# Converting the first weight's float64 words: two VectorE operations and a sign matmul in place of three VectorE operations

## The chip, the cores and the metric

The kernel runs on one core of a Trainium2 chip. The metric is device time in microseconds (us) of one execution. The profiler's span, from the first to the last instruction, is a little shorter than that time. Engines are named as in the profile: PE is TensorE, DVE VectorE, ACT ScalarE, POOL GpSimd and SP SyncE.

## The reference

Attention over B=4 batches, H=8 heads, S=768 positions and D=64, with a local window of 96 positions, 8 global keys and a linear distance bias, followed by a two-layer feed-forward net on the 3072 token rows:

```python
scores = scale * np.matmul(q, k.transpose(0, 1, 3, 2))
keep = is_global | is_local
dist = np.where(is_global & ~is_local, float(n_local), np.abs(rel))
scores = np.where(keep, scores - slopes * dist, -1e9)
a = softmax(scores); x = np.matmul(a, v)            # (3072, 512)
h = x @ w_in                                        # w_in: 512 x 2048
g = np.where(h >= 1, h, np.where(h <= -1, 0, (h + 1) ** 2 / 4))
out = g @ w_out                                     # w_out: 2048 x 512
```

The weights w_in and w_out arrive as float64, everything else as float32.

## The kernel before, in words

**Weights.** Each weight comes in 16 pieces of 512 KB, loaded as pairs of 32-bit words (`w_load`, three raw buffers). `w_bits` makes float32 words of them on VectorE in three operations on 128x512 tiles: line 430 takes the high word, masks it and shifts it left by three, into a PSUM tile; line 436 takes sign and top exponent bit from the high word and ors them in; line 439 shifts the low word right by 29 and ors it in, into the SBUF tile `w_f`. Then ScalarE writes a scaled float16 high half (`w_hi`, line 452), ScalarE scales `w_f` in place (`w_scale`, line 458), and GpSimd subtracts the half from it, which leaves the low half (`w_lo`, line 463). The halves are `wih`, `wil` (w_in) and `woh`, `wol` (w_out). The matmuls run on such pairs of halves.

**Attention.** A unit is 128 rows of one batch, a half unit four of its heads. The first row block of every batch (four units) is done in float32 by the `first_*` functions. The later ones use float16 pairs: `conv_hi`, `conv_lo` (lines 710 and 711 on GpSimd) split q, k and v; line 757 does the scores on TensorE; line 560 adds bias and takes the extreme on VectorE (`masked`, 128x256, or 128x128 in the first units); line 573 does the exponential on ScalarE; lines 774 and 776 split the result into `ph`; a transposing DMA brings `ph` to `pt`; line 801 multiplies with v; line 630 normalises into `xs`. Lines 740 and 742 copy the global keys and values.

**Feed-forward.** A chunk is 256 token rows (two units). `ffn1` (line 936) is the first product, three matmuls of 256 columns for each 128x128 weight block; `gelu` (lines 1011 to 1024) is the activation, split in halves; `ffn2` (line 1047) is the second product, three matmuls of 512 columns for each piece of w_out (a triple). Chunks 0 and 1 are made of the four first units, chunk 2 of the units 4 and 5. Later chunks use a seven-product scheme (line 973) with mixed weights (`tsum`, `tt`) and mixed inputs (`xa`).

**Fillers.** `filler` (line 400, tiles `spare_*`) multiplies zeros into a free PSUM tile. Its result is not used.

**What sets the order.** Each engine runs its instructions in the order in which the program issues them. Every piece of work is entered in a list by `at(t, ...)`, and the table `PLACE` gives the place of each entry in the final order, by hand. `after(...)` only asserts that what a piece of work needs has been issued ahead of it. Tiles come from pools: in PSUM `ps_s` has 2 buffers, `ps_av` 1, `ps_h` 3 and `ps_o` 2; the words of `w_bits`, the fillers and the outputs of the products share `ps_h` and `ps_o`. The sixteen pieces of w_in are converted ahead of those of w_out. ffn1 of chunk 0 starts when the first pieces of w_in are done.

Of the kernel before, what the change touches and what calls it, by code (L numbers as in the profile page):

```python
# [9 lines left out]
F16 = mybir.dt.float16  # L10
# [41 lines left out]
CPRE = 0  # L52
PRODUCTS = ("p1", "p5", "p2", "p6", "p3", "p7", "p4")
NFILL = 90
WS = "d"
# [218 lines left out]
def fast_path(ctx, tc, q, k, v, nraw, nval, w_in, w_out, out, half, nm, rr, sq, worst, badi):  # L274
# [109 lines left out]
    def slope(own, h):  # L384
# [6 lines left out]
        if h % 4 == 0:  # L391
            obias[h // 4] = ttp.tile([P, 4, P], F32, tag="t", name=f"obias{h // 4}")
# [49 lines left out]
    def signed(n):  # L442
        return WS[n % len(WS)] == "s"

# [21 lines left out]
    def put_weight(n, t, tl):  # L466
# [4 lines left out]
        if signed(n):  # L471
            at(t + 2.7, w_sign, n)
            t += 1.2
# [923 lines left out]
```

## Time and profile before

| what | value |
|---|---|
| time, median of 3 runs | 616.25 us (614.4 to 617.4) |
| time of the profiled execution | 616.34 us |
| span of the profiled execution | 614.1 us |
| TensorE busy | 593.3 us, 97% |
| VectorE busy | 479.7 us, 78% |
| ScalarE busy | 425.8 us, 69% |
| GpSimd busy | 362.0 us, 59% |
| mean granted clock of TensorE | 0.997 |

The busy shares are means over stages with different limits, so a stage is read from its own stretch of the trace. Matmuls overlap in a row: their pitch, from start to start, is shorter than their busy time. The page's chain of the work that ended last holds a single step here (ScalarE's last output copy), so the limits are read from the windows, the groups of lines and the timeline.

### The profile page before, as it was taken

Reading aid. Unit: us, or ns where it says so; the run is one execution under the profiler, and the core shown is the slowest. Engines: PE = TensorE matmul, PEld = TensorE weight load, DVE = VectorE, ACT = ScalarE, POOL = GpSimd, SP = SyncE. Lnnn points to the kernel's source line nnn. Section 1 sums busy time; section 2 is a strip of 40 time slices with the busy share of each in tenths; the row PEclk is TensorE's granted clock in tenths of the full one; section 3 lists DMA queues with packets and bytes.
Section 4 is the critical chain, followed back from the end, with each engine's and each line's share of the span. In section 5 each row is a group of like instructions: output and inputs, shape, how many; then the busy total and the mean of one; then the engine's idle time right before and its main releaser. Section 6 shows DMA issues by size and latency. Waiting matters only on the chain. (4 is left out here: it accounts for less than half of the span.)

```text
span 614.1 us, 17482 instructions
## 1 busy us (share of the span) xinstructions
PE 593.3 (97%) x6990; PEld 426.4 (69%) x6990; DVE 479.7 (78%) x1187; ACT 425.8 (69%) x865; POOL 362.0 (59%) x369
## 2 busy tenths in 40 slices
PE   5999899998999999999999999999999999999997
PEld 3677687444884777876766866776876877777865
DVE  6799999989885797797879778878788788752570
ACT  3688688688885877987568767768777766653431
POOL 0156869969999986486348447258458345324220
PEclk9999899999999999999999999999999999999999
DMA  9454256795575537788859677687698596162001
GB/s 306 137 174 157 74 192 158 232 256 105 139 153 127 127 88 124 177 159 202 185 140 225 196 175 180 164 185 171 191 187 191 139 191 126 41 88 44 19 19 36
DMA packets 158984, 91.74 MB, mean 149 GB/s; under 512 B 122932, under 2 KB 139572, under 8 KB 158900
## 3 DMA queue, kind: packets, MB, share of 16 engines
q1 hardware_dynamic: 158896, 90.60, 61.6%
q8 instruction: 55, 0.90, 0.6%
q14 instruction: 29, 0.24, 0.1%
q10 hardware_dynamic: 4, 0.00, 0.0%
HBM read 54.53 MB, written 6.29 MB: 99 GB/s over the span
## 5 line engine op out<-in xcount | busy, mean ns | idle before, releaser
L1024 POOL TENSOR_TENSOR gl<-u,gh 128x512 f16<-128x512 f32 x88 | 110.8, 1265 | 110.4 <-ACT gh L1022 108.4
L1047 PE MATMUL o<-woh,gh 128*128 128x512 f16 (+1 forms) x368 | 136.3, 370 | 0.0
L1047 PE MATMUL o<-woh,gl 128*128 128x512 f16 (+1 forms) x368 | 136.1, 370 | 0.0
L1047 PE MATMUL o<-wol,gh 128*128 128x512 f16 (+1 forms) x368 | 136.1, 370 | 0.0
L973 PEld LDWEIGHTS <-tt 128*128 128x128 f16 x1728 | 100.3, 98 | 10.0
L1047 PEld LDWEIGHTS <-gh 128*128 128x128 f16 x736 | 65.9, 98 | 58.0
L573 ACT ACTIVATE z<-z,nm 128x256 f32<-128x256 f32 (+1 forms) x192 | 85.3, 480 | 15.0 <-DVE nm L560 15.0
L560 DVE CUSTOM_DVE_ANT_0 z<-s,bias 128x256 f32<-128x256 f32 x160 | 64.8, 413 | 17.8 <-PE s L757 17.8
L1022 ACT ACTIVATE gh<-u 128x512 f16<-128x512 f32 x88 | 54.6, 625 | 25.2 <-DVE u L1015 24.7
L973 PEld LDWEIGHTS <-wih 128*128 128x128 f16 x864 | 66.9, 98 | 4.5 <-DVE u L1015 0.3
L936 PE MATMUL h<-xt,wih 128*128 128x256 f16 x384 | 65.5, 277 | 4.1 <-DVE w_f L439 3.4
L1047 PEld LDWEIGHTS <-gl 128*128 128x128 f16 x368 | 36.0, 98 | 40.0
L776 DVE SCALAR_TENSOR_TENSOR ph<-z,ph 128x1024 f16<-128x1024 f32 x40 | 54.3, 1356 | 7.4 <-DMA pt<-ph 3.6
L936 PE MATMUL h<-xt,wil 128*128 128x256 f16 x192 | 53.1, 276 | 0.0
L494 DVE TENSOR_REDUCE sq<-c_raw 128x1 f32<-128x256 f32 x128 | 48.0, 407 | 1.8 <-DMA c_raw<-in_moe_w_out_dram 1.3
L936 PEld LDWEIGHTS <-wih 128*128 128x128 f16 x384 | 37.8, 99 | 10.4 <-issue 4.0
L973 PEld LDWEIGHTS <-wil 128*128 128x128 f16 x432 | 42.3, 98 | 0.0
L774 ACT ACTIVATE ph<-z 128x1024 f16<-128x1024 f32 x40 | 41.9, 1048 | 0.3
L463 POOL TENSOR_TENSOR wil<-w_f,wih 128x512 f16<-128x512 f32 x16 | 18.7, 1171 | 38.8 <-ACT w_f L458 38.8
L801 PEld LDWEIGHTS <-pt 128*128 128x128 f16 x960 | 34.2, 97 | 9.4 <-DMA pt<-ph 2.9
L973 PE MATMUL h_0a<-xtb,tt 128*128 128x128 f16 x648 | 40.6, 219 | 0.0
L973 PE MATMUL h_1a<-xtb,tt 128*128 128x128 f16 x648 | 40.6, 219 | 0.0
(178 smaller groups left out, 1349.7 us busy)
## 6 DMA issues: line engine op xcount, KB each, us to landing
w_raw<-in_moe_w_in_dram SPq DMA_DIRECT2D x16, 512.0 KB, 4.0
w_raw<-in_moe_w_out_dram SPq DMA_DIRECT2D x16, 512.0 KB, 4.5
c_raw<-in_moe_w_in_dram SPq DMA_DIRECT2D x32, 256.0 KB, 4.0
c_raw<-in_moe_w_out_dram SPq DMA_DIRECT2D x32, 256.0 KB, 3.6
kr<-in_k_dram SPq DMA_DIRECT2D x28, 256.0 KB, 3.9
vr<-in_v_dram SPq DMA_DIRECT2D x28, 256.0 KB, 3.6
qr<-in_q_dram SPq DMA_DIRECT2D x24, 256.0 KB, 4.2
out_dram<-ob SPq DMA_DIRECT2D x23, 256.0 KB, 2.1
```

Of the source, the lines that this page charges most:

```text
L463: nc.gpsimd.tensor_sub(lo, wf[n], hi)
L494: nc.vector.tensor_reduce(sq[:, col : col + 1], r, axis=AX.X, op=op, apply_absolute_value=True)
L560: nc.vector.tensor_tensor_reduce(out=p32[u, hf][:, hh, :], in0=pts[u, hf][hh // 2][:, hh % 2, 0:n], in1=obias[hf][:, hh, :] if own else bi ...
L573: nc.scalar.activation(z, z, AF.Exp, bias=nm[:, c : c + 1], scale=-1.0, **acc)
L774: nc.scalar.activation(ph, zf, AF.Copy, scale=SP_)
L776: nc.vector.scalar_tensor_tensor(ph, zf, SP_, phs[u, hf, 0], op0=ALU.mult, op1=ALU.subtract)
L801: nc.tensor.matmul(av[:, hh, :], pt[:, a, hh, kt, :], vt[:, c, 4 * hf + hh, :], start=(n == 0), stop=(n == 5),)
L936: nc.tensor.matmul(hp[:, e, :], w[:, dc, f], xt[:, a, dc, :], start=(n == 0), stop=(n == 3 * NDC - 1))
L973: nc.tensor.matmul(hp[:, m, :], w, xf(b, dc), start=(fresh and m == n == 0), stop=(m == 3 and n == 5), skip_group_check=not fresh,)
L1022: nc.scalar.activation(gt[c, g][0], us[c, g], AF.Copy)
L1024: nc.gpsimd.tensor_sub(gt[c, g][1], us[c, g], gt[c, g][0])
L1047: nc.tensor.matmul(os_[c, t][x], a[:, cs], w[:, f, ms], start=(n == 0 and i == 0), stop=(n == NFC - 1 and i == 2))
```

## The change

For the 16 pieces of w_in:

- ScalarE takes the sign of the raw high word, read as float32, into a float16 tile (`w_sign`, line 430 of the changed kernel). TensorE multiplies it by a constant matrix `twos`, -2 on the diagonal (`w_twos`, line 434), so that the PSUM tile holds the word of -2.0 or +2.0. One VectorE operation shifts the high word left by three and xors the PSUM word in (line 442). The final operation is as before (line 452 there).
- The in-place scaling moves from ScalarE to GpSimd (line 466 there).

The pieces of w_out keep their three operations and ScalarE's scaling. The table PLACE is new throughout, with 27 filler entries in the program where 86 stood. The ones column of a value block may be written ahead of its halves (`v_block`), and the mixing of inputs asks for its low half only where it uses it.

```diff
-CPRE = 0
+TWOS = range(16)
+PSCALE = range(16)
-WS = "d"
...
+        nc.vector.tensor_scalar(twos, ident, -2.0, None, op0=ALU.mult)
...
+    def bits_tile(n):
+        num, src, hi, lo = piece(n)
+        p, tag = (ps_o, "o") if num < NFC and num % 2 >= BODD else (ps_h, "h")
+        wbits[n] = p.tile([P, *hi.shape[1:]], F32, tag=tag, name=f"w{num}_bits")
+        return wbits[n]
+
+    def w_sign(n):
+        num, src, hi, lo = piece(n)
+        wsgn[n] = ggp.tile([P, *hi.shape[1:]], F16, tag="g", name=f"w{num}_sign")
+        nc.scalar.activation(wsgn[n], wraw[n][:, :, :, 1].bitcast(F32), AF.Sign)
+
+    def w_twos(n):
+        after("positions")
+        nc.tensor.matmul(bits_tile(n), twos, wsgn[n], start=True, stop=True)
+
     def w_bits(n, s):
...
+        t = (bits_tile(n) if s == 0 and n not in TWOS else wbits[n]).bitcast(I32)
+        if s == 0 and n in TWOS:
+            nc.vector.scalar_tensor_tensor(t, rh, 3, t, op0=ALU.logical_shift_left, op1=ALU.bitwise_xor)
+            did.add(("bits", n, 1))
+        elif s == 0:
             nc.vector.tensor_scalar(t, rh, 0x07FFFFFF, 3, op0=ALU.bitwise_and, op1=ALU.logical_shift_left)
...
     def w_scale(n):
...
+        if n in PSCALE:
+            nc.gpsimd.tensor_scalar(wf[n], wf[n], SW, 1.0, op0=ALU.mult, op1=ALU.mult)
+        else:
+            nc.scalar.activation(wf[n], wf[n], AF.Copy, scale=SW)
...
     def put_weight(n, t, tl):
         at(tl, w_load, n)
+        if n in TWOS:
+            at(t - 0.6, w_sign, n)
+            at(t, w_twos, n)
+        at(t + 0.1, w_bits, n, 0)
+        if n not in TWOS:
+            at(t + 1.13, w_bits, n, 1)
         at(t + 2.63, w_bits, n, 2)
```

**VectorE at a piece of w_in, among the first units.** Before, the three operations of a piece stand apart, with other work between:

```order
L430 TENSOR_SCALAR w4_bits_463<-w4_raw_357 128x512
L630 TENSOR_TENSOR xs0_284<-av1_1_454,rr_68 128x256
L436 SCALAR_TENSOR_TENSOR w4_bits_463<-w4_raw_357,w4_bits_463 128x512
L430 TENSOR_SCALAR w6_bits_482<-w6_raw_416 128x512
L653 TENSOR_TENSOR xt0_310<-xtp1_1_478,xt0_310 128x2x128
L583 TENSOR_SCALAR rr_68<-sums_122 128x4
L439 SCALAR_TENSOR_TENSOR w4_f32_501<-w4_raw_357,w4_bits_463 128x512
```

Now (line 442 is the xor, line 452 the final operation):

```order
L641 TENSOR_TENSOR xs0_315<-av1_0_442,rr_68 128x256
L442 SCALAR_TENSOR_TENSOR w5_bits_459<-w5_raw_401,w5_bits_459 128x512
L452 SCALAR_TENSOR_TENSOR w5_f32_474<-w5_raw_401,w5_bits_459 128x512
L600 RECIPROCAL rr_68<-rr_68 128x4
L664 TENSOR_TENSOR xt0_326<-xtp1_0_480,xt0_326 128x2x128
L442 SCALAR_TENSOR_TENSOR w7_bits_492<-w7_raw_437,w7_bits_492 128x512
L452 SCALAR_TENSOR_TENSOR w7_f32_510<-w7_raw_437,w7_bits_492 128x512
```

(The names carry the piece, w4 for piece 4.) The and-shift and the and-or of a piece have become one operation, and the final operation, which needs its result, now stands directly behind it.

**TensorE ahead of the first matmul of ffn1.** Before (line 400 is a filler, line 598 a transpose, line 936 ffn1):

```order
L400 MATMUL spare_o10_490<-zeros_120 128x512
L400 LDWEIGHTS zeros_120
L400 MATMUL spare_h21_492<-zeros_120 128x512
L400 LDWEIGHTS zeros_120
L400 MATMUL spare_o11_494<-zeros_120 128x512
L598 MATMUL tp2_0_496<-ident_119,z2_0_406 128x128 x4
L936 LDWEIGHTS wih_114
L936 MATMUL h0_0_508<-xt0_310,wih_114 128x256
```

Now (line 434 is the matmul of signs by twos, lines 558 and 625 scores and products with v of the first units, line 950 ffn1):

```order
L434 LDWEIGHTS twos_121
L434 MATMUL w6_bits_554<-w6_sign_522,twos_121 128x512
L558 MATMUL s3_1_0_559<-kr3_463,qr3_476 128x128
L558 MATMUL s3_1_1_560<-kr3_463,qr3_476 128x128
L558 MATMUL s3_1_0_559<-kr3_463,qr3_476 128x128
L558 MATMUL s3_1_1_560<-kr3_463,qr3_476 128x128
L625 MATMUL av2_0_566<-vr2_525,pt2_0_536 128x64 x4
L434 LDWEIGHTS twos_121
L434 MATMUL w8_bits_571<-w8_sign_552,twos_121 128x512
L950 LDWEIGHTS wih_114
L950 MATMUL h0_0_599<-xt0_326,wih_114 128x256
```

Where fillers stood ahead of ffn1, there are now two matmuls of signs, and scores and products with v.

**VectorE at the last piece of w_out.** Before (w30 is converted last; line 776 is the ph operation):

```order
L430 TENSOR_SCALAR w30_bits_2003<-w30_raw_1899 128x512
L560 ISA z6_0_1957,nm_67<-s6_0_1_1932,bias_118 128x256
L560 ISA nm_67 128x1
L436 SCALAR_TENSOR_TENSOR w30_bits_2003<-w30_raw_1899,w30_bits_2003 128x512
L586 TENSOR_SCALAR rr_68<-av5_0_2012 128x4
L776 SCALAR_TENSOR_TENSOR ph5_1_1_2068<-z5_1_1865,ph5_1_0_2010 128x1024
L589 RECIPROCAL rr_68<-rr_68 128x4
L740 COPY kh6_3_1794<-kg0_1234 128x8x32
L630 TENSOR_TENSOR xs2_1554<-av5_0_2012,rr_68 128x256
L560 ISA z6_1_2065,nm_67<-s6_1_0_2039,bias_118 128x256
L560 ISA nm_67 128x1
L439 SCALAR_TENSOR_TENSOR w30_f32_2102<-w30_raw_1899,w30_bits_2003 128x512
```

Now (lines 445, 448 and 452 are the three operations of a w_out piece):

```order
L571 ISA z7_1_2113,nm_67<-s7_1_1_2088,bias_118 128x256
L571 ISA nm_67 128x1
L571 ISA z7_1_2113,nm_67<-s7_1_1_2088,bias_118 128x256
L571 ISA nm_67 128x1
L445 TENSOR_SCALAR w30_bits_2185<-w30_raw_2116 128x512
L448 SCALAR_TENSOR_TENSOR w30_bits_2185<-w30_raw_2116,w30_bits_2185 128x512
L597 TENSOR_SCALAR rr_68<-av6_0_2138 128x4
L753 COPY kh7_4_1521<-kg0_486 128x8x32
L452 SCALAR_TENSOR_TENSOR w30_f32_2206<-w30_raw_2116,w30_bits_2185 128x512
```

The ph operation and the masks that stood between the operations of the last piece stand there no more, and the scores' masks of unit 7 stand ahead where those of unit 6 stood.

## Rows read from the trace of the kernel before

**Rows 1.** Part 1 of the page: busy us (share of the span) xinstructions

```profile
PE 593.3 (97%) x6990; PEld 426.4 (69%) x6990; DVE 479.7 (78%) x1187; ACT 425.8 (69%) x865; POOL 362.0 (59%) x369
```

**Rows 2.** Windows: us, PE, PEld, DVE, ACT, POOL busy, PEclk, DMA share, GB/s

```profile
0.00:33.00 33.00, 24.64 (x145) 16.81 (x146) 24.15 (x107) 18.50 (x58) 5.53 (x10) 1.00 0.67 217
154.20:614.10 459.90, 455.36 (x5873) 333.83 (x5871) 340.63 (x828) 310.40 (x597) 261.77 (x269) 1.00 0.62 140
```

**Rows 3.** Timeline, last w_out piece: start us, us, engine, line, operation [idle <-releaser]

```profile
143.32 0.68 DVE L439 SCALAR_TENSOR_TENSOR w_f<-w_raw,w_bits 128x512 int32<-128x512 int32 x1
145.56 1.59 POOL L710 TENSOR_SCALAR kr<-kr 128x512 f32<-128x512 f32 x1
150.25 1.56 POOL L463 TENSOR_TENSOR wol<-w_f,woh 128x512 f16<-128x512 f32 x1
151.86 0.38 PE L1047 MATMUL o<-wol,g 128*128 128x512 f16 x1 [0.37 <-POOL wol L463]
```

**Rows 4.** Windows up to the last word, then to its use

```profile
0.00:144.00 144.00, 129.45 (x1022) 88.04 (x1022) 130.07 (x336) 107.49 (x253) 90.14 (x92) 0.99 0.63 183
144.00:151.90 7.90, 6.20 (x89) 3.48 (x87) 6.73 (x20) 7.32 (x15) 7.82 (x10) 1.00 0.49 113
```

**Rows 5.** Lines, VectorE, 160 us: xcount | busy us, mean ns | idle

```profile
L436 DVE SCALAR_TENSOR_TENSOR w_bits<-w_raw,w_bits 128x512 int32<-128x512 int32 x32 | 22.0, 689 | 0.2
L430 DVE TENSOR_SCALAR w_bits<-w_raw 128x512 int32<-128x512 int32 x32 | 21.9, 688 | 3.9 <-PE spare_o L400 2.4 <-DMA w_raw<-in_moe_w_out_dram 1.3
L776 DVE SCALAR_TENSOR_TENSOR ph<-z,ph 128x1024 f16<-128x1024 f32 x6 | 9.6, 1606 | 0.3 <-ACT ph L774 0.3
L740 DVE COPY kh<-kg 128x256 f16<-128x256 f16 x4 | 2.9, 734 | 0.0
L630 DVE TENSOR_TENSOR xs<-av,rr 128x256 f32<-128x256 f32 x13 | 5.5, 420 | 2.3 <-PE av L614 2.1
```

**Rows 6.** Timeline of VectorE: three pairs of neighbours

```profile
27.91 0.69 DVE L430 TENSOR_SCALAR w_bits<-w_raw 128x512 int32<-128x512 int32 x1
28.51 0.28 DVE L560 CUSTOM_DVE_ANT_0 z<-s,obias 128x128 f32<-128x128 f32 x1
111.19 0.70 DVE L430 TENSOR_SCALAR w_bits<-w_raw 128x512 int32<-128x512 int32 x1
111.93 0.70 DVE L436 SCALAR_TENSOR_TENSOR w_bits<-w_raw,w_bits 128x512 int32<-128x512 int32 x1
135.48 0.42 DVE L560 CUSTOM_DVE_ANT_0 z<-s,bias 128x256 f32<-128x256 f32 x1
135.82 0.69 DVE L436 SCALAR_TENSOR_TENSOR w_bits<-w_raw,w_bits 128x512 int32<-128x512 int32 x1
```

**Rows 7.** Timeline of TensorE: four groups of matmuls

```profile
77.38 0.38 PE L936 MATMUL h<-xt,wih 128*128 128x256 f16 x2
144.61 0.84 PE L801 MATMUL av<-vh,pt 128*128 128x65 f16 x22 [0.51 <-DMA pt<-ph]
148.26 0.86 PE L757 MATMUL s<-kh,qh 64*128 64x128 f16 x24
152.08 0.59 PE L1047 MATMUL o<-woh,g 128*128 128x512 f16 x2
```

**Rows 8.** Windows of line 400, the fillers (PE, PEld, PEclk, DMA, GB/s)

```profile
0.00:62.80 62.80, 18.48 (x64) 6.56 (x64) 1.00 0.59 189
62.80:154.20 91.40, 6.78 (x23) 1.91 (x22) 0.98 0.66 171
```

**Rows 9.** Lines of GpSimd, first 160 us

```profile
L463 POOL TENSOR_TENSOR wil<-w_f,wih 128x512 f16<-128x512 f32 x16 | 18.7, 1171 | 38.8 <-ACT w_f L458 38.8
L710 POOL TENSOR_SCALAR kr<-kr 128x512 f32<-128x512 f32 x6 | 4.7, 787 | 0.0
```

**Rows 10.** TensorE around its longest wait: one row of the timeline, one window

```profile
71.45 0.38 PE L936 MATMUL h<-xt,wih 128*128 128x256 f16 x2 [2.16 <-DVE w_f L439]
72.00:75.00 3.00, 3.00 (x16) 0.50 0.63 175
```

More of the change, by code (lines that the diff above doesn't have):

```diff
@@ L315, in fast_path @@
     zeros = const.tile([P, P], F16, name="zeros")
+    twos = const.tile([P, P], F16, name="twos")
     jrow = bias[:, H - 1, :]
@@ L390, in slope @@
             return
-        if h % 4 == 0:
+        if h // 4 not in obias:
             obias[h // 4] = ttp.tile([P, 4, P], F32, tag="t", name=f"obias{h // 4}")
@@ L411, in piece @@
         return n, src, woh[:, f : f + 1, :], wol[:, f : f + 1, :]
-    wraw, wf, wbits = {}, {}, {}
+    wraw, wf, wsgn, wbits = {}, {}, {}, {}
     def w_load(n):
@@ L424, in w_bits @@
         rh, rl = r[:, :, :, 1], r[:, :, :, 0]
-        if s == 0:
-            p, tag = (ps_o, "o") if num < NFC and num % 2 >= BODD else (ps_h, "h")
-            wbits[n] = p.tile([P, *hi.shape[1:]], I32, tag=tag, name=f"w{num}_bits")
-        t = wbits[n]
-        if s == 0:
+        t = (bits_tile(n) if s == 0 and n not in TWOS else wbits[n]).bitcast(I32)
[3 more added lines that the diff above has]
+        elif s == 0:
             nc.vector.tensor_scalar(t, rh, 0x07FFFFFF, 3, op0=ALU.bitwise_and, op1=ALU.logical_shift_left)
-            did.add(("bits", n))
-        elif s == 1 and signed(n):
-            after(("bits", n))
-            nc.scalar.activation(rh.bitcast(F32), rh.bitcast(F32), AF.Sign)
         elif s == 1:
+            after(("bits", n, 0))
             nc.vector.scalar_tensor_tensor(t, rh, -0x40000000, t, op0=ALU.bitwise_and, op1=ALU.bitwise_or)
         else:
+            after(("bits", n, 1))
             f = mid.tile([P, *hi.shape[1:]], I32, tag="m", name=f"w{num}_f32")
@@ L440, in w_bits @@
             wf[n] = f.bitcast(F32)
-    def signed(n):
-        return WS[n % len(WS)] == "s"
-    def w_sign(n):
-        nc.gpsimd.tensor_tensor(wf[n], wf[n], wraw[n][:, :, :, 1].bitcast(F32), op=ALU.mult)
-        did.add(("sign", n))
+        did.add(("bits", n, s))
     def w_hi(n):
         num, src, hi, lo = piece(n)
-        after(("sign", n)) if signed(n) else None
+        after(("bits", n, 2))
         nc.scalar.activation(hi, wf[n], AF.Copy, scale=SW)
@@ L457, in w_scale @@
         did.add(("scale", n))
-        nc.scalar.activation(wf[n], wf[n], AF.Copy, scale=SW)
+        if n in PSCALE:
+            nc.gpsimd.tensor_scalar(wf[n], wf[n], SW, 1.0, op0=ALU.mult, op1=ALU.mult)
+        else:
+            nc.scalar.activation(wf[n], wf[n], AF.Copy, scale=SW)
     def w_lo(n):
@@ L467, in put_weight @@
         at(tl, w_load, n)
-        at(t, w_bits, n, 0)
-        at(t + 1.13, w_bits, n, 1)
+        if n in TWOS:
[4 more added lines that the diff above has]
+            at(t + 1.13, w_bits, n, 1)
         at(t + 2.63, w_bits, n, 2)
-        if signed(n):
-            at(t + 2.7, w_sign, n)
-            t += 1.2
         at(t + 2.79, w_hi, n)
@@ L678, in fetch, with v_block @@
         fetched[u, kind, j] = r
+    def v_block(b, j):
+        if (b, j) not in vblk:
+            vblk[b, j] = hp_.tile([P, 2, H, D + 1], F16, tag="v", name=f"vh{b}_{j}")
+        return vblk[b, j]
     def conv_hi(u, kind, j):
@@ L683, in conv_hi @@
         if kind == "v":
-            f = hp_.tile([P, 2, H, D + 1], F16, tag="v", name=f"vh{u}_{j}")
+            f = v_block(b, j)
             nc.scalar.activation(f[:, 0, :, 0:D], r.rearrange("p (a b) -> p a b", a=H), AF.Copy, scale=SV)
@@ L693, in conv_ones @@
         did.add(("one", b, j, e))
-        nc.gpsimd.memset(vblk[b, j][:, e, :, D : D + 1], 1.0 - e)
+        nc.gpsimd.memset(v_block(b, j)[:, e, :, D : D + 1], 1.0 - e)
     def conv_lo(u, kind, j):
@@ L706, in conv_lo @@
             return
-        if CPRE:
-            nc.scalar.activation(r, r, AF.Copy, scale=SQK)
-        else:
-            nc.gpsimd.tensor_scalar(r, r, SQK, 1.0, op0=ALU.mult, op1=ALU.mult)
+        nc.gpsimd.tensor_scalar(r, r, SQK, 1.0, op0=ALU.mult, op1=ALU.mult)
         nc.gpsimd.tensor_sub(f[:, 1, :], r, f[:, 0, :])
@@ L832, in mix_x @@
     def mix_x(c, n):
-        after(("xs", 2 * c + 1, 0), ("xs", 2 * c + 1, 1), ("xa", 2 * c, 1))
+        after(("xs", 2 * c + 1, 0), ("xs", 2 * c + 1, 1))
+        after(("xa", 2 * c, 1)) if n >= 2 else None
         after(("mix", c, n - 1)) if n else None
```

320 rows, old and new, of the table PLACE are left out of this document.

## The prediction, made before the changed kernel was run

> **What bounds the kernel now.** TensorE is busy 593.3 of the 614.1 us of the span [rows 1], so I first ask where its 20.8 idle us lie. After 154.2 us it is busy 455.36 of 459.90 [rows 2]: from there to the end the kernel is a stream of matmuls that waits for almost nothing, and only work moved ahead of that point, or an earlier arrival at it, can shorten it. All the rest of the idle time is ahead of it, and part of what counts as busy there is no work: 64 fillers before 62.8 us and 23 up to 154.2 us [rows 8] (86 stand in the order; one is cut by the window's edge). Their busy time overlaps. A group of two filler-sized matmuls takes 0.59 us and one takes 0.38 [rows 7], so each costs a pitch of 0.21, and 86 of them some 18 us.
>
> So what sets the arrival? I follow the last w_out piece. VectorE writes its last word at 143.32 + 0.68 = 144.0. GpSimd takes until 150.25 to start its low half, having other work first (a conversion of 1.59 us at 145.56), and TensorE uses it at 151.86, released by exactly that instruction [rows 3]. That is a lag of 7.8 us. Up to 144.0 VectorE is busy 130.07, so it idles 13.9, and in the stretch 144.0 to 151.9 TensorE is busy 6.20 of 7.9 [rows 4]. In the first 33 us VectorE idles 33 - 24.15 = 8.85 of these 13.9 [rows 2]. TensorE idles more there than VectorE in the whole run-in: 151.9 less 129.45 and 6.20 is 16.2 us [rows 4], with 18 us of fillers besides. **VectorE's list ahead of the last word is the bound of the first 150 us; TensorE is the bound after it.**
>
> **The change, part by part.**
>
> *Bits of w_in.* The and-shift (line 430) and the and-or (line 436) become one shift-xor on 16 pieces. Both old forms take 688 and 689 ns [rows 5]. The new one has the shape, types and operands of line 436 (one raw word, one PSUM word), so I give it that price. What an operation costs is its pitch: beside an independent neighbour 28.51 - 27.91 = 0.60 us, and 111.93 - 111.19 = 0.74 where the next one needs its result [rows 6]. Sixteen operations fewer: -16 x 0.60 = -9.6. The xor now often stands directly ahead of the final operation that needs it. I count 8 such pairs more than before, so 8 x 0.14 = +1.1. The constant is one 128x128 operation, +0.2. Sum on VectorE: **-8.3 us**.
>
> *What the new order puts ahead of the last word.* Counted over VectorE's order up to the last w_f: 32 masked scores of 128x256 where 21 stood, 11 x 0.34 (135.82 - 135.48) [rows 6] = +3.7; two more ph operations at 1606 ns [rows 5] = +3.2; one more kh copy, 0.7, one more xs product, 0.4 [rows 5], and one vh copy fewer with some reciprocals more, which cancel within 0.3. Sum **+7.6 to +8.0**. So the last word comes only 8.3 - 7.6 = 0.7 us earlier at equal idle time. The gain of the bit operations is spent on doing attention work earlier.
>
> *What TensorE then has behind it.* Ahead of the first use of the last low half stand 24 more ffn1 matmuls of 256 columns (a group of two lasts 0.38, one 0.27, as the neighbouring rows of that line do, so 0.11 each, 2.6), three more half units of scores (24 matmuls in 0.86 of which some 0.78 is pitch, 2.3), one half unit of attention times v (0.7, from 22 matmuls in 0.84) and two triples of ffn2 (6 x 0.21 = 1.3) [rows 7]. That is **7.0 us** of real work that need not be done after the arrival.
>
> *TensorE's new work.* 16 matmuls with twos, 512 columns at 0.21: +3.4. 59 fillers fewer: -12.4. Both lie in the run-in, where TensorE idles 16.2 us. I cost them at nothing. The cover is that idle time plus the 12.4; with 7.0 + 3.4 added and 12.4 taken away the run-in has even 2 us more room than now.
>
> *ScalarE and GpSimd.* ScalarE swaps 16 scalings for 16 sign operations of the same size, none on the net, but these now stand ahead of VectorE's xor instead of behind the word. GpSimd gets 16 scalings; the same form costs 787 ns as a mean [rows 9], so +11 to +12.6 us. It is busy 5.53 of the first 33 us [rows 2], and waits 38.8 us in all ahead of the 16 low halves of w_in [rows 9]. That wait hides them. Counted over its own order, about 19 us more work than before stands ahead of the last wol, these scalings included; it idles 144 - 90.14 = 53.9 by 144.0 [rows 4]. If that cover went, the low halves would come late one by one, and ffn1 would wait for them.
>
> What GpSimd may give back is on VectorE: L776 at 1606 ns here [rows 5] has a mean of 1356 in the whole kernel, and I read the excess as work beside a busy GpSimd. [...]
>
> *Sum.* -0.7 on VectorE's list and -7.0 of work done before it: -7.7, with VectorE's idle time (13.9) and the lag (7.8) kept. The profiled execution took 616.34 us (2.2 outside the span), beside a median of 616.25, so no correction is due: 616.34 - 7.7 = **608.6**. The two kept terms carry the uncertainty. The lag can fall to about 5 us, since in the new order one gelu half stands there instead of the conversion of 1.59 us [rows 3] and what follows it (-2.8), or stay. VectorE's idle time can go from 13.9 down to 8 (-6) or up to 22 (+8), because the early units now run in another order and the xor waits for two engines.
>
> **Rivals.**
> *B, VectorE's early idle time goes as well.* A single wait for a filler's PSUM tile, 2.4 us, is the largest piece [rows 5], and with 59 fillers gone that tile is free. With it and half the waits for av (2.1 in all [rows 5]) and a shorter lag, -5.5 more: **603**. Against: twos now takes the same PSUM tiles. 0.22.
> *C, the hand-offs eat the gain.* Sign, twos and xor are on three engines. The wait for av, 2.1 us in 6 times [rows 5], prices one such hand-off at 0.35 when it shows. 16 of these are 5.6, with some that queue behind other work, +8: **614 to 617**. For: ScalarE is in order, and its sign operations stand among exponentials that wait for VectorE. Against: the orders put sign and twos several instructions ahead. 0.14.
> *D, slower.* The same mechanism, with VectorE blocked in front of the xor because the sign is queued behind an exponential that waits for scores not yet made. It decides from 7.7/16 = 0.48 us a piece. At 1.0 us it costs 16 and gives **624**; slower by over 0.5% begins at 0.67 us a piece. 0.09.
> *E, the clock.* After a wait of 2.16 us at 71.45, TensorE shows a granted clock of 0.50, its 1.2 GHz level, for the whole of 72 to 75 us [rows 10], so matmuls took twice as long for 3 us, at a price of 1.5. Fillers keep it from idling, and 59 go. Two more such stretches in the run-in cost 3, where TensorE is late through them: **611 to 612**. 0.05. The Trainium skill, "TensorE: Matmul & The Clock Gate", section "HAM oscillation — how this bites in real kernels", tells of bursts of matmuls that each start at the lower clock after a wait for data; the trace agrees for the one stretch of rows 10.
> That the change does not do what it says (the two operations kept) is excluded by the order, where two stand per piece.
>
> **How the numbers follow.** Forecast A, 608.6, has 0.50, and its own range is 605 to 613. B 0.22, C 0.14, D 0.09, E 0.05. The measurement can tell some 0.5%, 3.1 us. Faster (below 613.2): A, B and E, 0.77. Same: C, 0.14. Slower (over 619.3): D, 0.09. The range 601 to 616 leaves out D, the top of C (0.03) and the bottom of B (0.06), together 0.18.
>
> **What would show it.** Right: the 16 xor operations near 690 ns; VectorE's last w_f at 143 or so; the first chunk that needs the last low half starting near 152, but with some 7 us less of TensorE work behind it; TensorE's fillers at 27. B: VectorE's idle time before its last word under 10 us. C or D: waits of the xor for TensorE's twos, summing to 5 us or over 10. E: stretches of 0.50 in TensorE's clock ahead of 150 us. I am wrong altogether if TensorE idles much more than 5 us after the last low half, or if GpSimd is what the first ffn1 chunks wait for.

## The result, and the profile after

The changed kernel takes 608.58 us (median of 4 runs, 606.0 to 608.85), the kernel before 615.33 us beside it (4 runs), a ratio of 0.9883 with a 95% interval of 0.9856 to 0.991. Run again beside the last experiments it took 609.83 us (7 runs, ratio 0.9921, 0.9892 to 0.9949); the median over all 11 runs is 608.85. The forecast was 608.6, faster by over 0.5%.

Its profiled execution took 608.85 us with a span of 607.0, 7.1 less than before. Part 1 of the page, the answer to [rows 1]:

```profile
PE 585.0 (96%) x6947; PEld 420.8 (69%) x6947; DVE 462.4 (76%) x1172; ACT 420.3 (69%) x865; POOL 374.9 (62%) x385
```

Windows of the changed kernel in the stretches of [rows 2] and around its own last word (columns: us, then PE, PEld, DVE, ACT and POOL busy, PEclk, DMA share, GB/s):

```profile
0.00:33.00 33.00, 28.34 (x175) 17.75 (x176) 26.98 (x125) 25.12 (x80) 15.15 (x26) 1.00 0.81 259
...
0.00:137.00 137.00, 124.71 (x1083) 85.08 (x1084) 126.21 (x351) 114.36 (x268) 105.58 (x114) 1.00 0.72 207
137.00:154.20 17.20, 15.70 (x185) 11.25 (x184) 11.82 (x31) 13.75 (x31) 16.89 (x16) 1.00 0.83 147
...
154.20:607.00 452.80, 444.58 (x5683) 324.49 (x5681) 324.40 (x793) 292.19 (x568) 252.45 (x257) 1.00 0.63 134
```

Timeline of the changed kernel at the last w_out piece, as in [rows 3] (line 452 writes the last word, line 473 subtracts the halves):

```profile
136.33 0.68 DVE L452 SCALAR_TENSOR_TENSOR w_f<-w_raw,w_bits 128x512 int32<-128x512 int32 x1
...
139.21 2.13 POOL L1038 TENSOR_TENSOR gl<-u,gh 128x512 f16<-128x512 f32 x1
141.31 1.15 POOL L473 TENSOR_TENSOR wol<-w_f,woh 128x512 f16<-128x512 f32 x1
```

The last word ends at 137.0, where it ended at 144.0, and its low half at 142.5 instead of 151.8. VectorE is busy 126.21 of the 137.0 us, so it idles 10.8 where it idled 13.9 [rows 4].

Now the ledger of TensorE up to 154.2 us. It idles 154.2 - 124.71 - 15.70 = 13.8 us, against 16.3 before. Line 400, the fillers, in the windows of [rows 8]:

```profile
0.00:62.80 62.80, 10.53 (x27) 2.75 (x27) 1.00 0.71 223
62.80:154.20 91.40, 0.00 (x0) 0.00 (x0) 1.00 0.75 185
```

At a pitch of 0.21, fillers took 18.1 us before and 5.7 now, and the 16 matmuls by twos take 3.4. What is left is other work: 154.2 - 16.3 - 18.1 = 119.8 before, 154.2 - 13.8 - 5.7 - 3.4 = 131.3 now, by estimate 11.5 us more. The estimate is rough, since in the kernel before a filler at 15.70 us took 0.63 us and the next one started 0.43 behind it. The windows behind 154.2 us give the same thing directly: 455.36 us busy before [rows 2], 444.58 now. **So TensorE has 10.8 us less to do behind 154.2 us.** There it idles 452.80 - 444.58 = 8.2 us, against 4.5. **There 3.7 us are given back**, and 10.8 - 3.7 = 7.1 is the difference of the spans. TensorE's waits from 154 us to the end (us in total, times, longest us) name 4.0 of the 8.2 us; before there was none over 1 us:

```profile
PE s L770 <- DVE nm L571: 2.0, 2, 1.7
PE h_0a L987 <- DMA xtb<-xb: 2.0, 1, 2.0
```

The second of them has a further price. It ends at 239.7 us, and shortly behind it TensorE shows a granted clock of 0.50, its 1.2 GHz level (us, PE busy, PEclk, DMA share, GB/s):

```profile
241.00:244.00 3.00, 3.00 (x13) 0.50 0.17 58
```

By the price of 1.5 us for the 3 us of [rows 10], this is an estimated 1.5 us more, and it is contained in the 444.58.

VectorE's operations in the first 160 us, as in [rows 5]:

```profile
L789 DVE SCALAR_TENSOR_TENSOR ph<-z,ph 128x1024 f16<-128x1024 f32 x9 | 14.2, 1576 | 0.8 <-ACT ph L787 0.8
...
L442 DVE SCALAR_TENSOR_TENSOR w_bits<-w_raw,w_bits 128x512 int32<-128x512 int32 x16 | 11.0, 689 | 1.8 <-PE w_bits L434 1.7
...
L753 DVE COPY kh<-kg 128x256 f16<-128x256 f16 x4 | 1.6, 389 | 0.0
```

The xor takes 689 ns. Its hand-off costs 1.7 us of VectorE's time in all, in 3 waits, and TensorE waits 1.9 us for the signs (first 155 us; us in total, times, longest us):

```profile
DVE w_bits L442 <- PE w_bits L434: 1.7, 3, 1.0
PE w_bits L434 <- ACT w_sign L430: 1.9, 5, 0.5
```

### The profile page after: what moved, and what is told of

The parts are those of the page before. It is cut to its first block, busy times and chain, and to the rows that moved or that the text cites. A ratio compares the mean times of both kernels' runs of the same rounds, so it can differ in the third digit from the quotient of the medians.

```text
span 607.0 us, 17486 instructions
## 1 busy us (share of the span) xinstructions
PE 585.0 (96%) x6947; PEld 420.8 (69%) x6947; DVE 462.4 (76%) x1172; ACT 420.3 (69%) x865; POOL 374.9 (62%) x385
## 4 chain that ended last, share of the span: by engine, by line
PE 73%; DVE 10%; POOL 5%; DMA 5%; ACT 3%; issue 3%; SPq 0%; DVEq 0%; POOLq 0%; ACTq 0%
PE o L1061 32%; PE h_0a L987 8%; PE h_1a L987 7%; PE h L950 4%; PE h_0b L987 4%; PE av L814 4%; PE s L770 3%; PE h_1b L987 3%; PE h_1c L987 2%; DMA w_raw<-in_moe_w_in_dram 2%; PE h_0c L987 2%; PE spare_h L400 1%; DVE ph L789 1%; POOL g L1038 1%; DVE z L571 1%
## 5 line engine op out<-in xcount | busy, mean ns | idle before, releaser
L1038 POOL TENSOR_TENSOR gl<-u,gh 128x512 f16<-128x512 f32 x88 | 109.3, 1251 | 135.0 <-ACT gh L1036 127.6
L584 ACT ACTIVATE z<-z,nm 128x256 f32<-128x256 f32 (+1 forms) x192 | 89.3, 482 | 16.0 <-DVE nm L571 15.6
L571 DVE CUSTOM_DVE_ANT_0 z<-s,bias 128x256 f32<-128x256 f32 x160 | 63.0, 414 | 9.1 <-PE s L770 7.9
L789 DVE SCALAR_TENSOR_TENSOR ph<-z,ph 128x1024 f16<-128x1024 f32 x40 | 59.4, 1484 | 10.9 <-ACT ph L787 7.1
L950 PE MATMUL h<-xt,wih 128*128 128x256 f16 x384 | 64.2, 273 | 1.9 <-DMA xt<-xa 1.5
L505 DVE TENSOR_REDUCE sq<-c_raw 128x1 f32<-128x256 f32 x128 | 49.6, 410 | 14.7 <-DMA c_raw<-in_moe_w_out_dram 9.3
L770 PE MATMUL s<-kh,qh 64*128 64x128 f16 x960 | 34.4, 217 | 3.7 <-DVE nm L571 3.6
```

The costliest lines, as they stand in the source:

```text
L505: nc.vector.tensor_reduce(sq[:, col : col + 1], r, axis=AX.X, op=op, apply_absolute_value=True)
L571: nc.vector.tensor_tensor_reduce(out=p32[u, hf][:, hh, :], in0=pts[u, hf][hh // 2][:, hh % 2, 0:n], in1=obias[hf][:, hh, :] if own else bi ...
L584: nc.scalar.activation(z, z, AF.Exp, bias=nm[:, c : c + 1], scale=-1.0, **acc)
L770: nc.tensor.matmul(pair[r][:, j, e * P : (e + 1) * P], qf[rows, a, 2 * hf + j, :], kf[rows, c, 2 * hf + j, :], start=(n == 0), stop=(n == 2),)
L789: nc.vector.scalar_tensor_tensor(ph, zf, SP_, phs[u, hf, 0], op0=ALU.mult, op1=ALU.subtract)
L950: nc.tensor.matmul(hp[:, e, :], w[:, dc, f], xt[:, a, dc, :], start=(n == 0), stop=(n == 3 * NDC - 1))
```

## The experiments

Three theories were tested. **1**: VectorE's list bounds the run-in, so that its 16 operations fewer are what counts. **2**: the new order alone brings the gain. **3**: the hand-off from ScalarE through TensorE to VectorE decides, and the places laid out between the three are what the change lives on. Each run is given by its median, and by its ratio to the kernel before on the same chip.

### Order and operations apart

The new order with the old operations:

```diff
-        nc.scalar.activation(wsgn[n], wraw[n][:, :, :, 1].bitcast(F32), AF.Sign)
...
-        nc.tensor.matmul(bits_tile(n), twos, wsgn[n], start=True, stop=True)
+        bits_tile(n)
...
-            nc.vector.scalar_tensor_tensor(t, rh, 3, t, op0=ALU.logical_shift_left, op1=ALU.bitwise_xor)
+            nc.vector.tensor_scalar(t, rh, 0x07FFFFFF, 3, op0=ALU.bitwise_and, op1=ALU.logical_shift_left)
+            nc.vector.scalar_tensor_tensor(t, rh, -0x40000000, t, op0=ALU.bitwise_and, op1=ALU.bitwise_or)
```

> The changed kernel's order with the three old VectorE operations for w_in (and-shift and and-or back to back where the xor stood; no sign operation, no matmul by twos; GpSimd still scales). Theory 1, VectorE's list up to the last word bounds the run-in: 16 operations more at 0.60 to 0.74 us, so the last word comes some 10 us later than the 137.0 us of the changed kernel and the time is 608.6 + 6 to 10 = 615 to 619 us. Theory 2, the new order alone brings the gain (work moved ahead, 59 fillers gone) and the two operations matter little: 607 to 610 us.

621.66 us (7 runs), ratio 1.0101 (1.0067 to 1.0135): 13 us above the changed kernel and slower than the one before. Theory 2 is out. But this run also took 16 matmuls from TensorE, and its clock fell. TensorE in three windows of that run (us, PE busy, PEclk, DMA share, GB/s):

```profile
18.00:24.00 6.00, 4.87 (x22) 0.52 0.64 214
36.00:42.00 6.00, 6.00 (x31) 0.50 0.52 159
70.00:72.00 2.00, 2.00 (x11) 0.50 0.61 180
```

So the next run keeps a matmul at each of the 16 places, of zeros:

```diff
-        bits_tile(n)
+        nc.tensor.matmul(
+            bits_tile(n).rearrange("p a b -> p (a b)").rearrange("p (a b) -> p a b", a=4),
+            zeros, zeros.unsqueeze(1).to_broadcast([P, 4, P]), start=True, stop=True,
+        )
```

> As the run with the new order and the three old operations (621.7 us), but with a matmul of zeros where the matmul by twos stood, its result overwritten; no sign operation. Theory 1 (VectorE's 16 more operations cost 10 us, the rest of the 13 us was TensorE's lower clock in three stretches): 616 to 619 us, with fewer windows at 0.50. Rival (the clock made most of the 13 us): 609 to 613 us. Rival (the clock nothing): 620 to 623 us.

619.48 us (6 runs), ratio 1.009 (1.0067 to 1.0114). Two of the three stretches are at full clock again, and one at 1.2 GHz remains:

```profile
18.00:24.00 6.00, 4.41 (x36) 1.00 0.71 229
36.00:42.00 6.00, 5.31 (x46) 1.00 0.46 146
66.00:72.00 6.00, 5.25 (x25) 0.50 0.29 87
```

The 16 VectorE operations are thus worth 619.48 - 608.85 = 10.6 us with that one stretch, which lies in the 9.6 to 11.8 of 16 x 0.60 to 0.74. The last word of w_out ends at 148.3 us in this run, 11.3 later than in the changed kernel:

```profile
147.65 0.69 DVE L454 SCALAR_TENSOR_TENSOR w_f<-w_raw,w_bits 128x512 int32<-128x512 int32 x1
```

Two things go with the 16 operations here, the stretch at 1.2 GHz and the absence of ScalarE's 16 signs; their shares were not separated. What the two other stretches cost the run before is not shown: its median is 2.2 us higher, with overlapping intervals.

The other way round, the new operations in the old order, sign and twos at the place of the and-shift, the xor at that of the and-or:

```diff
...
+        if s == 0 and n < NFC:
...
+            sgn = ggp.tile([P, *hi.shape[1:]], F16, tag="g", name=f"w{num}_sign")
+            nc.scalar.activation(sgn, rh.bitcast(F32), AF.Sign)
+            nc.tensor.matmul(wbits[n], twos, sgn, start=True, stop=True)
+        elif s == 1 and n < NFC:
+            nc.vector.scalar_tensor_tensor(t, rh, 3, t, op0=ALU.logical_shift_left, op1=ALU.bitwise_xor)
```

> The kernel before, in its own order with all its fillers, with sign, matmul by twos and xor in place of the and-shift and the and-or of w_in; sign and twos are issued where the and-shift stood, the xor where the and-or stood, ScalarE still scales. Theory 1 with cheap hand-offs: VectorE's list gets 8 us shorter, and 608 to 612 us come out. Theory 2 (the order is what counts): 614 to 617 us. Theory 3, hand-offs that nothing covers cost over 0.5 us a piece, since only one VectorE operation or so stands between sign and xor: 617 to 626 us, with waits of the xor for TensorE summing to 8 us or more.

624.42 us (6 runs), ratio 1.0156 (1.0127 to 1.0185), as theory 3 has it. The waits of VectorE in its first 155 us begin with

```profile
DVE w_bits L438 <- PE w_bits L435: 12.1, 10, 2.9
DVE xs L640 <- PE av L624: 5.3, 6, 2.3
```

ScalarE has both the signs and the scalings in this run, so the 9.5 us above the kernel before are not the order's alone.

### The distance between the three

The changed kernel with sign and twos issued directly ahead of the xor, where the PSUM tile of the word is now asked for too; nothing else moved:

```diff
     def w_sign(n):
...
-        nc.scalar.activation(wsgn[n], wraw[n][:, :, :, 1].bitcast(F32), AF.Sign)
+        return
 
     def w_twos(n):
-        after("positions")
-        nc.tensor.matmul(bits_tile(n), twos, wsgn[n], start=True, stop=True)
+        return
...
-        t = (bits_tile(n) if s == 0 and n not in TWOS else wbits[n]).bitcast(I32)
+        t = (bits_tile(n) if s == 0 else wbits[n]).bitcast(I32)
         if s == 0 and n in TWOS:
+            after("positions")
+            nc.scalar.activation(wsgn[n], rh.bitcast(F32), AF.Sign)
+            nc.tensor.matmul(wbits[n], twos, wsgn[n], start=True, stop=True)
             nc.vector.scalar_tensor_tensor(t, rh, 3, t, op0=ALU.logical_shift_left, op1=ALU.bitwise_xor)
```

> The changed kernel with sign and matmul by twos issued directly ahead of the xor in the program, all else in its place. If the distance laid out between the three hides the hand-offs, the waits of the xor for TensorE rise from 1.7 us in 3 to some 8 to 12 us in 10 or more, as in the run of the new operations in the old order (12.1 us), and the time is 613 to 620 us. If ScalarE and TensorE are early enough anyway: 608 to 610 us.

631.84 us (6 runs), ratio 1.0304 (1.0273 to 1.0335), 23 us above the changed kernel and more than I had expected at most. VectorE's longest entry in the waits, and TensorE's:

```profile
DVE w_bits L444 <- PE w_bits L443: 22.2, 14, 3.8
...
PE w_bits L443 <- ACT w_sign L442: 15.0, 12, 4.1
```

That is 22.2/16 = 1.4 us a piece, where 1.7/16 = 0.1 is what the laid-out places leave. TensorE's own wait for the sign, 15.0 us, shows that the larger part arises ahead of the matmul: in ScalarE's queue and in the sign itself, which takes 0.65 us. TensorE's clock falls with these waits. This is its mean from 33 to 62.8 us (us, then PE, PEld, DVE, ACT and POOL busy, PEclk, DMA share, GB/s), where the changed kernel has 1.00:

```profile
33.00:62.80 29.80, 21.50 (x142) 15.90 (x141) 16.49 (x47) 17.60 (x46) 15.03 (x16) 0.81 0.47 152
```

So the 23 us are the waits and the clock that fell through them, together. **The change without its distance is slower than the kernel before by 3%.**

### What the other engines got

Twos twice:

```diff
-        nc.tensor.matmul(bits_tile(n), twos, wsgn[n], start=True, stop=True)
+        b = bits_tile(n)
+        nc.tensor.matmul(b, twos, wsgn[n], start=True, stop=True)
+        nc.tensor.matmul(b, twos, wsgn[n], start=True, stop=True)
```

> The changed kernel with each of the 16 matmuls by twos done twice, which adds 16 x 0.21 = 3.4 us to TensorE, all of it before 63 us. The forecast's step (TensorE has room in the run-in, its new work costs nothing): within 1 us of 608.6. Theory 3, TensorE's own list bounds the run-in of the changed kernel: 611 to 612 us.

605.79 us (6 runs), ratio 0.9877 (0.9847 to 0.9908), within the interval of the changed kernel's 0.9883. 3.4 us more on TensorE cost nothing before 63 us: TensorE's own list does not bound that stretch.

The scalings back on ScalarE:

```diff
-PSCALE = range(16)
+PSCALE = ()
```

> The changed kernel with the scalings of w_in back on ScalarE, 16 x 0.53 = 8.5 us more on ScalarE in its first 65 us, where the changed kernel has it busy 52.8 of 62.8, and 10 us less on GpSimd. Theory 1 (VectorE is the bound and only what blocks it counts): signs and exponentials come later by up to a few us, 609 to 614 us, with longer waits of the matmul by twos for ScalarE. Rival (ScalarE is nowhere near the path, GpSimd is): 606 to 609 us.

611.98 us (12 runs), ratio 0.9975 (0.9959 to 0.9991). The interval lies above both of the changed kernel's, and the median is 3 us higher. The largest of TensorE's waits there is the matmul by twos for the sign, which was 1.9 us in 5 times:

```profile
PE w_bits L434 <- ACT w_sign L430: 4.5, 5, 1.8
```

That fits later signs, but does not show them as the cause: the same wait is 3.3 and 4.0 us in the traces of the last two runs below, which leave ScalarE's work as it is.

A second scaling by 1.0 behind each on GpSimd:

```diff
             nc.gpsimd.tensor_scalar(wf[n], wf[n], SW, 1.0, op0=ALU.mult, op1=ALU.mult)
+            nc.gpsimd.tensor_scalar(wf[n], wf[n], 1.0, 1.0, op0=ALU.mult, op1=ALU.mult)
```

> The changed kernel with a second scaling, by 1.0, behind each of the 16 on GpSimd: 16 x 0.7 = 11 us more on GpSimd before 63 us. The forecast's step (GpSimd's waits hide what it gets): within 2 us of the changed kernel beside it. Rival (GpSimd has become tight, with 35 of 63 us busy more than planned and the low halves queued): 4 to 11 us more, with waits of ffn1 for low halves.

611.28 us (12 runs), ratio 0.9952 (0.9924 to 0.998), 1.5 us above the changed kernel beside it with intervals that overlap. GpSimd hides most of 11 us more; whether the rest costs anything is not shown.

### Fillers

In both kernels `filler` returns at once:

```diff
     def filler(tag, n):
+        return
```

> The changed kernel without its 27 fillers. Theory 1 (TensorE has room until 62.8 us, where all 27 lie): within 1 us of 608.6. The clock's theory: TensorE idles in the first 30 us, runs first units and first chunks at 1.2 GHz, and the time is 610 to 613 us, with windows of granted clock 0.50 in the first 60 us. A theory in which TensorE's own list bounds the run-in: 27 x 0.21 = 5.8 us less, 603 us.

> The kernel before without its 86 fillers. Theory 1 (VectorE's list bounds the run-in, fillers stand in idle time): 614 to 618 us, no gain from 18 us less on TensorE. The clock's theory: stretches at 1.2 GHz, 617 to 622 us. A theory in which the fillers themselves delay what VectorE waits for (PSUM tiles of 2.4 us, TensorE's queue): 609 to 613 us.

The changed kernel without its 27: 610.18 us (8 runs), ratio 0.9917 (0.9888 to 0.9945), not told from the changed kernel's 0.9883 and 0.9921, though one stretch of TensorE ahead of 154 us is at 1.2 GHz:

```profile
32.00:38.00 6.00, 6.00 (x28) 0.50 0.60 181
```

The kernel before without its 86: 621.48 us (6 runs), ratio 1.0109 (1.0087 to 1.0132), slower by 6.5 us. TensorE's clock is 0.50 in two stretches, and VectorE waits longer for TensorE than the 2.1 us of [rows 5]:

```profile
70.00:72.00 2.00, 2.00 (x11) 0.50 0.03 8
152.00:158.00 6.00, 4.26 (x31) 0.50 0.68 153
```

```profile
DVE xs L631 <- PE av L615: 6.2, 7, 2.0
```

Fillers were worth their place in the old order. In the new one they can go without a cost that can be told. That the matmuls by twos do a part of their work is seen in the two runs with the old operations, where zero matmuls at the same places left one of three stretches; that the work moved ahead does the rest is argued, not shown.

### What binds the changed kernel

The changed kernel itself, beside the next ones:

> The changed kernel itself, as the measure for the two runs beside it: 606 to 609 us.

609.83 us. Its runs lie between 604.3 and 611.69, wider than the kernel before (612.34 to 618.23). Its profiled execution was a short one, with a span of 602.5 us; TensorE was busy 143.57 us up to 154.2 there, 3.2 more than in the first. The mean granted clock goes with the time: of the eleven runs of the changed kernel, the five at 0.996 or more took 604.3 to 608.85 us, and the six at 0.990 to 0.994 took 608.58 to 611.69. The kernel before, beside the later seven, had 0.997 to 1.000. So a part of the changed kernel's gain may be lost to the clock in many executions; this was not tried.

Two moves in the table, meant to take away the two waits behind 154 us:

```diff
...
+    for moved, ahead in (((1527, 1535, 1543), 1503), ((1698,), 1707)):
+        place = [n for n in place if n not in moved]
+        at_ = place.index(ahead)
+        place[at_:at_] = moved
...
```

> The changed kernel with two moves in its table behind the run-in: three ffn2 triples of chunk 3 ahead of the product that waits 2.0 us for a transposed input (237.5 us), and the transpose of one ph half of unit 12 issued ahead of that unit's other half, so that VectorE does not wait 3.2 us for its buffer and the scores not 1.7 us for the masks (271.8 us). If these two waits give back a part of what the run-in gained, TensorE being busy otherwise from 154 us on: 3 to 4 us less than the changed kernel beside it, and both waits gone from the trace. If something else holds the stream (TensorE's wait only moves to the next piece): within 1 us of it.

607.49 us (6 runs), ratio 0.9888 (0.9849 to 0.9927). One wait is gone; the other is not. VectorE still idles 3.2 us there ahead of the ph operation, and the profile still puts that down to a transposing DMA of `ph`, so the move did not take away what it waits for; what that is stays open. TensorE's waits from 154 us on:

```profile
PE s L770 <- DVE nm L571: 1.9, 1, 1.9
```

2.3 us below the changed kernel beside it, with overlapping intervals: not shown to be faster.

The final operation of the last two words done five times:

```diff
-            nc.vector.scalar_tensor_tensor(f, rl, 29, t, op0=ALU.logical_shift_right, op1=ALU.bitwise_or)
+            for _ in range(5 if n >= 30 else 1):
+                nc.vector.scalar_tensor_tensor(f, rl, 29, t, op0=ALU.logical_shift_right, op1=ALU.bitwise_or)
```

> The changed kernel with the final VectorE operation of the last two pieces of w_out (30 and 31, at 133.5 and 136.3 us) done five times in place of once: 8 x 0.6 to 0.7 = 5 us more on VectorE there, what stands behind it included. The forecast's chain (the last word of w_out sets the arrival) holds for the changed kernel as well: 5 us more than the 608.9 us at which its runs so far have their median, 613 to 615 us. Rival (in the changed kernel the last word is early, and what binds the run-in is VectorE's list in the w_in part, where 16 operations more cost 11 us): within 2 us, 607 to 611 us, with the lag from the last word to its use shorter by about 5 us.

612.57 us (12 runs), ratio 0.9973 (0.9948 to 0.9999), 3.7 us above the median of the changed kernel: between the two expectations. The trace says in part how. TensorE does not wait for the low half of the late words. It waits for the normalised product that VectorE has behind them, as this timeline of VectorE and then TensorE shows:

```profile
141.50 3.58 DVE L453 SCALAR_TENSOR_TENSOR w_f<-w_raw,w_bits 128x512 int32<-128x512 int32 x5
145.00 0.17 DVE L601 RECIPROCAL rr<-rr 128x4 f32<-128x4 f32 x1
145.27 0.42 DVE L642 TENSOR_TENSOR xs<-av,rr 128x256 f32<-128x256 f32 x1
```

```profile
145.84 0.96 PE L815 MATMUL av<-vh,pt 128*128 128x65 f16 x24 [2.60 <-DVE xs L642]
```

So in the changed kernel VectorE's list can hold TensorE up through whatever stands in it: 16 operations in the w_in part cost 10.6 us, and eight at its end came with 3.7 us more. The last word of w_out is no longer the place where one sees it.

The list is not all. The sign waits for the raw words of its piece, a link that the prediction did not name. ScalarE's sign near 41 us, in the changed kernel, in the run with two moves and in the last one:

```profile
40.33 0.67 ACT L430 ACTIVATE w_sign<-w_raw 128x512 f16<-128x512 f32 x1 [0.39 <-DMA w_raw<-in_moe_w_in_dram]
41.67 0.66 ACT L430 ACTIVATE w_sign<-w_raw 128x512 f16<-128x512 f32 x1 [2.47 <-DMA w_raw<-in_moe_w_in_dram]
42.18 0.66 ACT L430 ACTIVATE w_sign<-w_raw 128x512 f16<-128x512 f32 x1 [3.13 <-DMA w_raw<-in_moe_w_in_dram]
```

In the last run TensorE then waits 3.02 us for this sign and falls to 1.2 GHz:

```profile
44.00:47.50 3.50, 3.50 (x20) 0.52 0.54 138
```

The edits of both runs lie far behind that point. The run-in thus differs from one execution to the next by when raw words land, and a part of the time that the last trace lost was lost here and not through its edit. Why the words land later was not tried.

## Why the prediction was right, point by point

- **VectorE's operations: right.** The xor has line 436's price (689 ns), and undoing it costs 10.6 us (one stretch at 1.2 GHz included) where the two kinds of pitch give 9.6 to 11.8.
- **"The last word comes only 0.7 us earlier": wrong.** It came 7.0 us earlier. The masks (32, +3.6 us busy) and the two ph operations more (+3.2) cost what I had said. But I priced the rest of the list at its old durations, and VectorE's busy time up to the last word fell by 130.07 - 126.21 = 3.9 us. Six operations that build the 128x256 distance table alone went from 5.4 to 2.4 us (last section), and the kh copies of [rows 5] from 734 to 389 ns each; others went the other way, as the eight on the sums of the first units (lines 583 and 594), from 2.0 to 4.0 us. VectorE's idle time fell by 3.1, about half of rival B.
- **"7.0 us of real work moved ahead", the lag kept: a sum with a wrong split.** With that list and 59 fillers gone, TensorE had 10.8 us less to do behind 154.2 us, where the sum had 7.7. The lag of 7.8 us, which I had kept, is no quantity of the new kernel: the last low half lies ready at 142.5 us, and no matmul from 126 us on waits for one.
- **Missing: the 3.7 us given back.** Two waits at 237.5 and 271.8 us, in the part of the table behind the run-in. I had taken the stream behind 154 us as unchanged. The two errors, 3.1 and 3.7 us, cancel to 0.6; the size is right by luck to within them, the sign and the bound of the run-in by the argument. One sign of being wrong came near: TensorE idles 8.2 us behind the last low half, where the prediction allowed not much more than 5.
- **TensorE's new work at nothing: right** (3.4 us more cost nothing). **GpSimd's wait as cover: right** (11 us more cost about 1.5, not told from nothing). What I did not say is that ScalarE could not have kept the scalings for nothing: 3 us.
- **Rivals C and D.** The mechanism is real and larger than I allowed. It costs 12.1 us of waits in the old order, with ScalarE's scalings beside it, and 22.2 in the new one without distance, 1.4 us a piece, far beyond the 0.67 at which I let slower begin. I gave D 0.09 because sign and twos stand several instructions ahead, and that is exactly what decides.
- **Rival E: in another place.** In the two traces of the changed kernel no window of TensorE from 0 to 154 us shows a lowered clock, though fillers fell to 27; taking the rest away as well gives one such stretch there. But it falls behind 154 us, at 241 us in the first trace and from 266 to 271 in the second (mean 0.66), and six of the eleven runs have a lower mean than these two; where it falls in those is not shown. I had looked at the run-in alone. (The wait of [rows 10] is not TensorE's longest in the kernel before: two of 2.41 us stand in its first 10 us.)

## What to carry to other kernels

Moving a piece of a busy engine's work to two others paid here only with its place on each of them laid out ahead by the time that their queues take: the same operations gave -1.2% and -0.8% in two comparisons with that distance and +3% without it. Price a list of instructions at the durations that it will have beside its new neighbours, not at its old ones. And when a stretch gets shorter, look for what it gives back later, in waits and in the clock behind them, in a part that nobody meant to change.

## What the runs showed of the hardware

The same VectorE operations on 128x256 float32 tiles took 1.7 to 3.3 times as long beside a GpSimd that ran almost without a break. In the kernel before, GpSimd is busy from 58.8 us on and this is VectorE:

```profile
61.06 1.14 DVE L362 TENSOR_SCALAR m<-bias,prow 128x256 f32<-128x256 f32 x1
65.56 1.26 DVE L380 SCALAR_TENSOR_TENSOR m<-m,nval 128x256 f32<-128x256 f32 x1
```

In the changed kernel GpSimd idles for 2.10 us ahead of 54.25 and for 1.35 ahead of 56.42, and the same two lines, which fall into these pauses, are

```profile
53.06 0.35 DVE L362 TENSOR_SCALAR m<-bias,prow 128x256 f32<-128x256 f32 x1
55.42 0.48 DVE L380 SCALAR_TENSOR_TENSOR m<-m,nval 128x256 f32<-128x256 f32 x1
```

The run with the second scaling adds work to GpSimd alone. There GpSimd is busy 7.03 of the 7.48 us from the first to the last of the six operations, and they take 6.0 us in all instead of 2.4; line 380 is back at its old time:

```profile
58.24 1.25 DVE L380 SCALAR_TENSOR_TENSOR m<-m,nval 128x256 f32<-128x256 f32 x1
```

The xor, with one operand in PSUM, lay between 675 and 697 ns in all its 16 places. The Trainium skill, "SBUF — State Buffer", section "Who interferes with whom", states that VectorE operations with two SBUF inputs contend with a GpSimd instruction that reads SBUF, that forms such as tensor_scalar can take the port pair that both engines share, and that those with at most one SBUF input, outside the modes that use both ports, do not contend. The trace agrees with these rows: line 380 here has two SBUF inputs, line 362 is a tensor_scalar, and the xor has one SBUF input.
